# Attention in a float32 kernel: row maxima two heads at a time, sums in spare columns, reciprocals in quarters

## The chip, the cores and the metric

One core of one Trainium2 chip. The metric is the device time of one execution in microseconds; the kernel before has a median of 1218.71 us over three runs (1218.32 to 1220.46).

## What is computed

Attention over 4 batches of 8 heads with queries pooled in pairs, then a gated MLP that mixes positions, then a second MLP behind a low-rank mix of positions. The change lies in the attention:

```python
def _attn_ref(q, k, v) -> np.ndarray:
    B, H, S, D = q.shape          # 4, 8, 1152, 64
    q_pool = q.reshape(B, H, S // 2, 2, D).mean(axis=3)
    scores = (1.0 / np.sqrt(D)) * np.matmul(q_pool, k.transpose(0, 1, 3, 2))
    scores = scores - np.max(scores, axis=-1, keepdims=True)
    attn = np.exp(scores)
    attn = attn / (np.sum(attn, axis=-1, keepdims=True) + 1e-09)
    return np.matmul(attn, v).astype(np.float32)
```

The weights of the MLPs arrive in float64 (w_spatial in float32) and are turned into pairs of float32 parts, high and low, by the kernel itself, during the attention.

## The kernel before, in words

The 32 heads are 16 pairs, and the 576 pooled queries of a pair of heads are two halves of 256 and 320: 32 jobs `u`, in order. A job goes over 9 chunks of 128 keys. Scores are made transposed, keys on the partitions: `scores(u, c)` (L180) writes a tile of two banks, one for each head, with q and k in full float32; `less` (L190) adds the negated row maximum by a matmul with a row of ones; `expo` (L201) exponentiates on ACT (L206) and adds the result up over the chunks on POOL (L211, tile `acc`); `pv` (L215) multiplies with V on PE into one bank for the job. At the end of a job `sums(u)` (L227) sums `acc` over the partitions by matmuls with ones, ACT copies that to SBUF (L238), `recip` (L240) takes the reciprocal on DVE in two halves, `out` (L245) multiplies and stores.

The maximum of a query must be known before its scores are made, so a second, rounded product q k is made ahead of it: `piece()` (L141) is one matmul (L147, 384 keys of one head, 128 queries) into one of the two banks of the pool `ring`, and one maximum over its 384 columns on DVE (L151). Six of them make 128 queries of two heads; a last small minimum (L154) joins them. `to_rows(u)` (L158) turns the columns of maxima into rows by transposing matmuls (L168) into both ring banks, from which ACT copies them (L173, L178). `sums` takes a ring bank too.

Banks of PSUM: 2 for the ring, 2 for the outputs of PV, 2 tiles of 2 for the scores.

The order is written by hand and every engine goes through its own part of it in order. The loop at L277 has 144 groups of two chunks (`G = 2`), nine groups to a pair of heads. A group is: up to two pieces (`some(2)`, L292), scores of both chunks, `less` and `expo` of both, up to two pieces again (L304) or, in the last group before a new job, all pieces that the job still needs and `to_rows` (L298 to L302), PV of the group before, then what is left of an ended job (L311: the sums and the first half of the reciprocal two groups after its last chunk, the second half and the output three groups after), then `also(i)`. `end` (L286) bounds the pieces: `AHEAD` of them ahead of an even rate.

`also(i)` runs one tick of `Weights` (L353): from group 8 on, every sixth group begins one unit of a weight, and each unit does one step a group for seven groups: two activations on ACT (L439, L440), then on DVE L444 and L446, on POOL L448, on DVE L450, then the copy to the high part (L460) and the subtraction for the low part (L465). The strings of `CFG` (L914) give the engines of the last two for each unit: first letter for the subtraction (v DVE, p POOL), second for the copy (v DVE, a ACT). A float32 unit has only these two steps.

After the loop come PV and the sums of the last job, then the two MLPs.

## Time and profile before

| | |
|---|---|
| median of three runs | 1218.71 us |
| the profiled execution's own time | 1220.57 us |
| its span, first to last instruction | 1218.8 us |
| granted clock of PE, mean of full speed | 0.986 |
| PE busy | 1164.7 us (96%) |
| DVE, ACT, POOL busy | 646.3, 438.8, 558.3 us |

The rows below come from the profiled execution. A row of a timeline has the start in us from the start of the span, the duration, the engine (PEld is PE's weight load), the line of the kernel, the operation, the tiles out<-in, the shapes and a count, since neighbours of one kind are merged; in brackets stands the idle time before it and the work whose end ended it. In a group by line stand the count, busy us, mean ns of one, and the idle time before them. The tile `yh` in some rows is room that the rounded q and k and the maxima borrow from a later stage.

### The profile page before, as it was taken

The numbers are of one execution on the slowest core, as the hardware profiler recorded it, in microseconds if no ns is written. First come the engines' busy times: TensorE is split into PE (matmuls) and PEld (weight loads), VectorE is DVE, ScalarE is ACT, GpSimd is POOL, SyncE is SP. The second block draws the span as 40 slices with busy tenths as digits, with TensorE's granted clock in tenths as the row PEclk, the third lists the DMA queues.
The fourth block names the chain that finished last, engine by engine and source line by source line (L and its number), as shares of the span: only waits on it lengthen the run. The fifth ranks groups of instructions, "written<-read, shape, count | busy, mean of one in ns | idle before, by whom it ended". The sixth has DMA issues, their size and how long they took to land.

```text
span 1218.8 us, 18185 instructions
## 1 busy us (share of the span) xinstructions
PE 1164.7 (96%) x7116; PEld 912.9 (75%) x7116; DVE 646.3 (53%) x1158; ACT 438.8 (36%) x868; POOL 558.3 (46%) x458
## 2 busy tenths in 40 slices
PE   7999999999999999999999999789999999999998
PEld 5665656566656555558998989579999999999997
DVE  4677767776777776745434333989852112121211
ACT  2444445444454444444333333555521111111110
POOL 3787878878778877773424243634310000000000
PEclk7999999999999999999999999989999999999999
DMA  6242223223333320001111103624400101010000
GB/s 155 79 106 72 76 82 88 79 79 96 86 99 115 80 59 30 26 15 54 44 40 39 49 1 129 189 98 133 136 27 26 52 1 52 1 52 1 27 1 27
DMA packets 37768, 79.17 MB, mean 65 GB/s; under 512 B 5553, under 2 KB 17841, under 8 KB 37682
## 3 DMA queue, kind: packets, MB, share of 16 engines
q1 hardware_dynamic: 37682, 78.01, 21.6%
q8 instruction: 56, 0.92, 0.3%
q14 instruction: 30, 0.25, 0.1%
HBM read 63.31 MB, written 14.16 MB: 64 GB/s over the span
## 4 chain that ended last, share of the span: by engine, by line
PE 50%; DVE 4%; DMA 0%; ACT 0%; issue 0%; POOL 0%; ACTq 0%; DVEq 0%
PE ph L1006 16%; PE py L1020 16%; PE pu L758 4%; PE pv L623 4%; PE pg L776 4%; PE py L806 3%; DVE w L465 1%; DVE st L450 1%; PE pV L831 1%; PE pt L998 1%; PE pU L792 1%; DVE st L444 1%; DVE st L446 0%; DMA raw<-in_moe_w_ch_dram 0%; DVE yh L345 0%
## 5 line engine op out<-in xcount | busy, mean ns | idle before, releaser
L211 POOL TENSOR_TENSOR acc<-acc,pt 128x512 f32<-128x512 f32 (+1 forms) x222 | 318.1, 1433 | 96.0 <-ACT pt L206 85.3
L151 DVE TENSOR_REDUCE m<-r 128x1 f32<-128x384 f32 x480 | 250.3, 550 | 103.1 <-PE r L147 98.0
L206 ACT ACTIVATE pt<-s 128x512 f32<-128x512 f32 (+1 forms) x288 | 171.6, 648 | 246.5 <-PE s L195 225.2
L1020 PE MATMUL py<-w,h 128*128 128x512 f32 x864 | 218.4, 397 | 1.9 <-ACT h L1009 1.4
L1006 PE MATMUL ph<-ut,w 128*128 128x384 f32 x1152 | 218.4, 338 | 0.0
L1006 PEld LDWEIGHTS ph<-ut,w 128*128 128x128 f32 x1152 | 205.5, 188 | 8.5
L1010 DVE SCALAR_TENSOR_TENSOR h<-ph,h 128x384 fp32r<-128x384 f32 x96 | 53.5, 557 | 267.2 <-ACT h L1009 267.1
L1020 PEld LDWEIGHTS py<-w,h 128*128 128x128 f32 x864 | 160.5, 189 | 32.6 <-ACT h L1009 1.7
L186 PE MATMUL s<-q,k 64*128 64x320 f32 (+1 forms) x1152 | 176.4, 412 | 0.4 <-ACT pt L206 0.4
L222 PE MATMUL po<-pt,v 128*64 128x320 f32 (+1 forms) x1152 | 171.7, 419 | 0.0
L147 PE MATMUL r<-yh 64*128 64x384 f32 x480 | 149.5, 431 | 21.3 <-DVE m L151 11.8
L1009 ACT ACTIVATE h<-ph 128x384 fp32r<-128x384 f32 x96 | 47.2, 491 | 310.9 <-PE ph L1006 310.9
L147 PEld LDWEIGHTS r<-yh 64*128 64x128 f32 x480 | 70.9, 188 | 113.0 <-DVE m L151 73.7
L186 PEld LDWEIGHTS s<-q,k 64*128 64x128 f32 x1152 | 117.2, 189 | 13.0 <-ACT pt L206 2.6
L222 PEld LDWEIGHTS po<-pt,v 128*64 128x64 f32 x1152 | 70.0, 136 | 51.1 <-issue 21.6
L195 PE MATMUL s<-toprow,yh 64*128 64x256 f32 (+1 forms) x576 | 100.7, 405 | 0.0
L243 DVE RECIPROCAL sum<-sum 128x128 f32<-128x128 f32 (+1 forms) x64 | 66.8, 1047 | 52.3 <-ACT sum L238 52.3
L448 POOL TENSOR_TENSOR st<-st,raw 128x512 int32<-128x512 int32 (+3 forms) x48 | 68.8, 1435 | 53.2 <-DVE st L446 43.3
L195 PEld LDWEIGHTS s<-toprow,yh 64*128 64x128 f32 x576 | 64.6, 190 | 11.7 <-issue 0.4
L776 PE MATMUL pg<-wst,vn 128*128 128x288 f32 x448 | 60.1, 295 | 0.0
L776 PEld LDWEIGHTS pg<-wst,vn 128*128 128x128 f32 x448 | 59.6, 188 | 0.0
L211 POOL TENSOR_TENSOR acc<-pt 128x512 f32<-128x512 f32 (+1 forms) x32 | 46.6, 1455 | 25.0 <-ACT pt L206 25.0
(117 smaller groups left out, 1131.2 us busy)
## 6 DMA issues: line engine op xcount, KB each, us to landing
raw<-in_moe_w_ch_dram SPq DMA_DIRECT2D x32, 512.0 KB, 3.8
k<-in_k_dram SPq DMA_DIRECT2D x32, 288.0 KB, 4.5
qraw<-in_q_dram SPq DMA_DIRECT2D x32, 288.0 KB, 5.8
v<-in_v_dram SPq DMA_DIRECT2D x16, 576.0 KB, 4.5
xn<-x SPq DMA_DIRECT2D x4, 1152.0 KB, 5.7
out_dram<-un SPq DMA_DIRECT2D x18, 256.0 KB, 2.1
raw<-in_moe_w_in_dram SPq DMA_DIRECT2D x8, 512.0 KB, 4.6
u<-o SPq DMA_DIRECT2D x16, 256.0 KB, 2.0
```

The lines of the kernel that those rows point to most:

```text
L147: nc.tensor.matmul(r, s["qr"][p, q0:q0 + 128], s["kr"][p, PW * i:PW * i + PW], start=True, stop=True)
L151: nc.vector.tensor_reduce(out=m[:, e, i:i + 1], in_=r, axis=AX.X, op=ALU.max, negate=True)
L186: nc.tensor.matmul(t[:, e, 0:n], s["k"][p, 128 * c:128 * c + 128], s["q"][p, q0:q0 + n], start=True, stop=False)
L195: nc.tensor.matmul(jb["s", c][:, e, 0:n], first[p], jb["top"][p, 0:n], start=False, stop=True)
L206: nc.scalar.activation(x[:, :, 0:n], t[:, :, 0:n], ACTF.Exp, scale=SC)
L211: nc.gpsimd.tensor_tensor(out=a, in0=jb["p", 0][:, :, 0:n] if c == 1 else a, in1=x[:, :, 0:n], op=ALU.add)
L222: nc.tensor.matmul(jb["o"][D * e:D * e + D, 0:n], st[u // 2]["v"][:, e, c], x[:, e, 0:n], start=c == 0, stop=c == KC - 1,)
L243: nc.vector.reciprocal(out=t, in_=t)
L448: nc.gpsimd.tensor_tensor(out=o, in0=o, in1=lo, op=ALU.add)
L776: nc.tensor.matmul(p[:, 0:HT], vn[:, a, s, 128 * m:128 * m + 128], wst[:, c, s, sl], start=s == 0 and i == 0, stop=s == NT - 1 and i == 1,)
L1006: nc.tensor.matmul(p[:, 0:BT], w1s[m][:, a, k], ut[i][:, c, k], start=j == 0, stop=j == 3 * KD - 1)
L1020: nc.tensor.matmul(py[i][c], h[:, a, 128 * c:128 * c + 128], w2s[m][:, e], start=m == 0 and a + e == 0, stop=m == KM - 1 and a == 1,)
```

## The change

One piece is now both heads: two matmuls into a tile of two banks, and one maximum over both (two heads by 384 columns). The ring has one such tile; before the loop the pieces rotate through it and the two score tiles. The transposes of the maxima go into one such tile, and one ACT copy takes both halves. `AHEAD` is 5 pieces of the new kind.

The order within a group: the transposes (and missing pieces), or else one piece; small work of an ended job; scores, `less`, `expo`; one piece; small work; PV; sums; `also`. The sums go into columns 320 and up of the group's second score tile, in two halves of the queries, one a bank, so with twice as many matmuls of half the width. The reciprocal is done in quarters, two in each of the third and fourth group after the last chunk; the output comes in the fifth.

All strings of `CFG` say `pa`: every subtraction on POOL, every copy on ACT (`V0` is not touched).

```diff
--- before.py
+++ after.py
@@ -58,13 +58,13 @@
 
     G = 2
 
-    AHEAD = 7
+    AHEAD = 5
 
     with ExitStack() as ctx, ExitStack() as sco:
         pt_p = ctx.enter_context(tc.tile_pool(name="pt_p", bufs=8))
         ld2 = ctx.enter_context(tc.tile_pool(name="ld2", bufs=2))
         ld = sco.enter_context(tc.tile_pool(name="ld", bufs=2))
-        ring_p = ctx.enter_context(tc.tile_pool(name="ring", bufs=2, space=PSUM))
+        ring_p = ctx.enter_context(tc.tile_pool(name="ring", bufs=1, space=PSUM))
         ps_o = ctx.enter_context(tc.tile_pool(name="ps_o", bufs=2, space=PSUM))
         ps_s = sco.enter_context(tc.tile_pool(name="ps_s", bufs=2, side="right", space=PSUM))
 
@@ -129,27 +129,28 @@
             nc.scalar.copy(s["kr"][:, c0:c1], s["k"][:, c0:c1])
 
         def ring(name):
-            return ring_p.tile([128, 512], F32, tag="r", name=name)
-
-
-        pieces = [
-            (u, c, i, e) for u in range(NJ) for c in range(len(HALF[u % 2][2])) for i in range(NPC) for e in range(2)
-        ]
-        upto = [sum(len(HALF[w % 2][2]) for w in range(u)) * NPC * 2 for u in range(NJ + 1)]
+            return ring_p.tile([128, 2, 512], F32, tag="r", name=name)
+
+
+        pieces = [(u, c, i) for u in range(NJ) for c in range(len(HALF[u % 2][2])) for i in range(NPC)]
+        upto = [sum(len(HALF[w % 2][2]) for w in range(u)) * NPC for u in range(NJ + 1)]
         done = [0]
 
-        def piece():
-            u, c, i, e = pieces[done[0]]
+        def piece(r=None):
+            u, c, i = pieces[done[0]]
             done[0] += 1
             s, q0 = st[u // 2], HALF[u % 2][2][c]
-            p = slice(D * e, D * e + D)
-            r = ring("r")[:, 0:PW]
-            nc.tensor.matmul(r, s["qr"][p, q0:q0 + 128], s["kr"][p, PW * i:PW * i + PW], start=True, stop=True)
-            if i == 0 and e == 0:
+            r = ring("r") if r is None else r
+            for e in range(2):
+                p = slice(D * e, D * e + D)
+                nc.tensor.matmul(
+                    r[:, e, 0:PW], s["qr"][p, q0:q0 + 128], s["kr"][p, PW * i:PW * i + PW], start=True, stop=True
+                )
+            if i == 0:
                 jobs[u]["m"] = ld.tile([128, 2, NPC], F32, tag="m", name="m", bufs=4)
             m = jobs[u]["m"]
-            nc.vector.tensor_reduce(out=m[:, e, i:i + 1], in_=r, axis=AX.X, op=ALU.max, negate=True)
-            if i == NPC - 1 and e:
+            nc.vector.tensor_reduce(out=m[:, :, i], in_=r[:, :, 0:PW], axis=AX.X, op=ALU.max, negate=True)
+            if i == NPC - 1:
                 t = tops[u // 2 % 2][c + 2 * (u % 2)]
                 nc.vector.tensor_reduce(
                     out=t.rearrange("p (e d) -> p e d", e=2)[:, :, 0], in_=m, axis=AX.X, op=ALU.min
@@ -160,22 +161,21 @@
             h = u % 2
             n = HALF[h][1]
             t = jobs[u]["top"] = ld.tile([128, NMAX], F32R, tag="toprow", name="toprow")
-            rs = [ring(f"tr{i}") for i in range(2)]
+            rs = ring("tr")
             for c in range(3 if h else 2):
                 for i in range(2):
                     if c < 2 or i:
                         p = slice(64 * i, 64 * i + 64)
                         nc.tensor.matmul(
-                            rs[i][:, 64 * c:64 * c + 64], tops[u // 2 % 2][c + 2 * h][p], idr[p, p],
+                            rs[:, i, 64 * c:64 * c + 64], tops[u // 2 % 2][c + 2 * h][p], idr[p, p],
                             start=True, stop=True,
                         )
-            for i in range(2):
-                nc.scalar.copy(
-                    t[:, 0:256].rearrange("p (c i x) -> p i c x", c=2, i=2)[:, i],
-                    rs[i][:, 0:128].rearrange("p (c x) -> p c x", c=2),
-                )
+            nc.scalar.copy(
+                t[:, 0:256].rearrange("p (c i x) -> p i c x", c=2, i=2),
+                rs[:, :, 0:128].rearrange("p i (c x) -> p i c x", c=2),
+            )
             if n > 256:
-                nc.scalar.copy(t[:, 256:n], rs[1][:, 128:192])
+                nc.scalar.copy(t[:, 256:n], rs[:, 1, 128:192])
 
         def scores(u, c):
             s = st[u // 2]
@@ -224,22 +224,26 @@
                     start=c == 0, stop=c == KC - 1,
                 )
 
-        def sums(u):
+        def sums(u, r, at):
+
             jb = jobs[u]
-            n = HALF[u % 2][1]
-            r = ring("ps")
+            n = HALF[u % 2][1] // 2
             terms = [jb["p", c] for c in range(added(u), KC)] + [jb["acc"]]
-            for i, x in enumerate(terms):
-                for e in range(2):
-                    nc.tensor.matmul(
-                        r[D * e:D * e + D, 0:n], ones, x[:, e, 0:n], start=i == 0, stop=i == len(terms) - 1
-                    )
+            for h in range(2):
+                for i, x in enumerate(terms):
+                    for e in range(2):
+                        nc.tensor.matmul(
+                            r[D * e:D * e + D, h, at:at + n], ones, x[:, e, n * h:n * h + n],
+                            start=i == 0, stop=i == len(terms) - 1,
+                        )
             t = jb["sum"] = ld2.tile([128, NMAX], F32, tag="sum", name="sum")
-            nc.scalar.activation(t[:, 0:n], r[:, 0:n], ACTF.Copy, bias=1e-9)
+            nc.scalar.activation(
+                t[:, 0:2 * n].rearrange("p (h n) -> p h n", h=2), r[:, :, at:at + n], ACTF.Copy, bias=1e-9
+            )
 
         def recip(u, i):
             n = HALF[u % 2][1]
-            t = jobs[u]["sum"][:, n * i // 2:n * (i + 1) // 2]
+            t = jobs[u]["sum"][:, n * i // 4:n * (i + 1) // 4]
             nc.vector.reciprocal(out=t, in_=t)
 
         def out(u):
@@ -259,21 +263,30 @@
 
         r = ring("warm")
         for i in range(WARM):
-            nc.tensor.transpose(r[:, 128 * (i % 4):128 * (i % 4) + 128], idf, idf)
+            nc.tensor.transpose(r[:, 0, 128 * (i % 4):128 * (i % 4) + 128], idf, idf)
         pool_q(0, nc.vector, 0, 256)
         round_q(0, 0, 256)
         round_k(0)
         pool_q(0, nc.gpsimd, 256, T)
         round_q(0, 256, T)
-        for _ in range(upto[1]):
-            piece()
+        for i in range(upto[1]):
+            piece(ps_s.tile([128, 2, 512], F32, tag="s", name="r0") if i % 3 else None)
         pool_q(1, nc.gpsimd)
         to_rows(0)
         chunks = [(u, c) for u in range(NJ) for c in range(KC)]
         groups = [chunks[i:i + G] for i in range(0, len(chunks), G)]
         PG = 2 * KC // G
         before = []
-        waiting = []
+
+        smalls = {}
+        sums_at = {}
+        for i, group in enumerate(groups):
+            for u, c in group:
+                if c == KC - 1 and u < NJ - 1:
+                    sums_at[i + 2] = u
+                    for n in range(4):
+                        smalls[i + 3 + n // 2, n % 2] = [lambda u=u, n=n: recip(u, n)]
+                    smalls[i + 5, 0] = [lambda u=u: out(u)]
         for i, group in enumerate(groups):
             j, r = divmod(i, PG)
             if r == 0:
@@ -285,37 +298,36 @@
 
             end = min(upto[1] + AHEAD + upto[2] * (i + 1) // PG, upto[NJ])
 
-            def some(n):
-                for _ in range(min(n, end - done[0])):
+            def some():
+                if done[0] < end:
                     piece()
 
-            some(2)
-            for u, c in group:
-                scores(u, c)
-            for u, c in group:
-                less(u, c)
-                expo(u, c)
             new = [u for u, c in (groups[i + 1] if i + 1 < len(groups) else ()) if c == 0]
             for u in new:
                 while done[0] < upto[u + 1]:
                     piece()
                 to_rows(u)
             if not new:
-                some(2)
+                some()
+            for x in smalls.pop((i, 0), ()):
+                x()
+            for u, c in group:
+                scores(u, c)
+            last = jobs[group[-1][0]]["s", group[-1][1]]
+            for u, c in group:
+                less(u, c)
+                expo(u, c)
+            some()
+            for x in smalls.pop((i, 1), ()):
+                x()
             if i + 1 == len(groups):
                 break
             for x in before:
                 pv(*x)
             before = group
 
-            for u, n in waiting:
-                if n == 1:
-                    sums(u)
-                    recip(u, 0)
-                if n == 2:
-                    recip(u, 1)
-                    out(u)
-            waiting = [(u, n + 1) for u, n in waiting if n < 2] + [(u, 0) for u, c in group if c == KC - 1]
+            if i in sums_at:
+                sums(sums_at[i], last, NMAX)
             also(i)
             if r == 4 and j + 2 < NP:
                 pool_q(j + 2, nc.gpsimd)
@@ -331,8 +343,10 @@
             pv(*x)
             for name in names.split():
                 also(name)
-        sums(NJ - 1)
-        for i in range(2):
+        for x in [x for k in sorted(smalls) for x in smalls[k]]:
+            x()
+        sums(NJ - 1, ring("ps"), 0)
+        for i in range(4):
             recip(NJ - 1, i)
         out(NJ - 1)
         for name in LEFT[G].split():
@@ -912,11 +926,11 @@
 
 
 CFG = dict(
-    EI="pa vv va pv va pv pa pa",
-    ES="va pa pa vv va",
-    EW="pa pv pv pa",
-    EU="pv pa",
-    EV="va pv",
+    EI="pa pa pa pa pa pa pa pa",
+    ES="pa pa pa pa pa",
+    EW="pa pa pa pa",
+    EU="pa pa",
+    EV="pa pa",
     V0="pv pv vv vv pa",
     END=[1, 3, 2, 2, 0, 2, 2, 1, 1, 3, 4, 2, 6],
     START="D D D D U D U n U n U n U n U n U n U n b U U U U U U U U U " + "X " * 9 + "G " * 17 + "P " * 9,
```

## Rows read from the trace of the kernel before

**Rows 1.** Stretch, us, busy us (instructions) of PE, PEld, DVE, ACT, POOL; clock, DMA.
```profile
53.41:521.62 468.21, 437.86 (x3181) 279.33 (x3181) 341.65 (x638) 219.25 (x424) 373.39 (x270) 1.00 0.29 81
```

**Rows 2.** Timeline, PE, first scores of a group: start, us, engine, line, operation.
```profile
255.34 1.02 PE L186 MATMUL s<-q,k 64*128 64x256 f32 x7
...
258.69 1.02 PE L186 MATMUL s<-q,k 64*128 64x256 f32 x8
...
262.50 1.13 PE L186 MATMUL s<-q,k 64*128 64x256 f32 x7
...
266.22 1.02 PE L186 MATMUL s<-q,k 64*128 64x256 f32 x8
...
270.09 1.13 PE L186 MATMUL s<-q,k 64*128 64x256 f32 x8
...
273.03 1.26 PE L186 MATMUL s<-q,k 64*128 64x320 f32 x8
...
276.26 1.24 PE L186 MATMUL s<-q,k 64*128 64x320 f32 x8
...
280.11 1.34 PE L186 MATMUL s<-q,k 64*128 64x320 f32 x7
...
286.69 1.02 PE L186 MATMUL s<-q,k 64*128 64x256 f32 x7
```

**Rows 3.** Timeline of a group 4, of the round from 286.69.
```profile
301.16 0.44 PE L147 MATMUL r<-yh 64*128 64x384 f32 x2
...
301.64 1.02 DVE L151 TENSOR_REDUCE m<-r 128x1 f32<-128x384 f32 x2 [2.00 <-PE r L147]
...
302.68 0.47 PE L147 MATMUL r<-yh 64*128 64x384 f32 x2
...
303.08 0.63 PEld L222 LDWEIGHTS po<-pt,v 128*64 128x64 f32 x8 [0.18 <-issue]
...
304.10 0.22 PEld L147 LDWEIGHTS r<-yh 64*128 64x128 f32 x2 [0.39 <-DVE m L151]
```

**Rows 4.** Timeline of groups 2 and 3 of that round.
```profile
294.89 2.05 DVE L151 TENSOR_REDUCE m<-r 128x1 f32<-128x384 f32 x4
...
295.44 0.18 PEld L147 LDWEIGHTS r<-yh 64*128 64x128 f32 x1 [0.27 <-DVE m L151]
...
299.70 0.52 PE L168 MATMUL tr<-yh 64*128 64x64 f32 x4 [0.36 <-DVE m L151]
```

**Rows 5.** Timeline at the end of its group 6: sums, then maxima.
```profile
310.37 0.60 PE L234 MATMUL ps<-acc,ones 128*64 128x256 f32 x4
...
310.90 0.99 PE L147 MATMUL r<-yh 64*128 64x384 f32 x2
...
311.45 0.18 PEld L147 LDWEIGHTS r<-yh 64*128 64x128 f32 x1 [0.37 <-ACT sum L238]
```

**Rows 6.** Groups of DVE by line, 50 to 535: xcount, busy us, mean ns, idle.
```profile
L151 DVE TENSOR_REDUCE m<-r 128x1 f32<-128x384 f32 x435 | 227.3, 550 | 89.3 <-PE r L147 85.8
L243 DVE RECIPROCAL sum<-sum 128x160 f32<-128x160 f32 x30 | 34.5, 1148 | 16.8 <-ACT sum L238 16.8
L243 DVE RECIPROCAL sum<-sum 128x128 f32<-128x128 f32 x29 | 27.5, 948 | 18.7 <-ACT sum L238 18.7
L450 DVE SCALAR_TENSOR_TENSOR st<-raw,st 128x512 int32<-128x512 int32 x12 | 16.6, 1384 | 2.4 <-POOL st L448 2.4
...
L446 DVE TENSOR_SCALAR st<-st 128x512 int32<-128x512 int32 x12 | 8.0, 669 | 0.0
L444 DVE TENSOR_SCALAR st<-st 128x512 f32<-128x512 f32 x12 | 7.9, 662 | 0.4 <-ACT st L439 0.4
L249 DVE TENSOR_TENSOR x<-po,sum 128x320 f32<-128x320 f32 x15 | 7.4, 492 | 0.5
```

**Rows 7.** Stretch 50 to 535: L465 on DVE and POOL; L460 on DVE and ACT.
```profile
50.00:535.00 485.00, 8.37 (x7) 16.42 (x16) 1.00 0.29 79
...
50.00:535.00 485.00, 6.63 (x9) 7.75 (x14) 1.00 0.29 79
```

## The prediction

> **What bounds the kernel now.** I read the busy time of whole stretches first [rows 1]. In 53.41 to 521.62 us, fourteen of the sixteen rounds of attention (a round is one pair of heads, nine groups of two key chunks), PE is busy for 437.86 of 468.21 us, POOL for 373.39 and DVE for 341.65. What follows attention is not touched by the change. So the time is PE's; what can be won are waits of PE inside attention, and a us won there moves everything behind it by a us.
>
> Next the timeline of PE alone, reduced to the first score matmul of each group [rows 2]. The round from 255.34 to 286.69, in which DVE does no weight work, takes 31.35 us; its groups 0 to 6 take 3.35, 3.81, 3.72, 3.87, 2.94, 3.23 and 3.85, groups 7 and 8 together 6.58. Group 4 has full work of its kind (four maxima, eight scores, eight PV) in 2.94, so 3.7 to 3.9 in groups 2 and 3 must hold waits. The timelines of such places name them. In group 2 four maxima queue on DVE behind half a reciprocal, and PE's weight load stands behind a maximum at 295.44; in group 3 the transposes of the maxima wait for them [rows 4]. In groups 1 and 6 the sums are made in one of the two banks of the maxima: the second maximum's matmul gets it only when ACT has copied them out, 0.55 us after the place where the sums ended [rows 5]. Over the fourteen rounds the mean is 468.21/14 = 33.44, 2.09 above the quiet round: weight work on DVE, put in front of maxima, costs 29 us in all.
>
> **The maxima.** Before: two matmuls into two banks, two maxima of 550 ns, 1.02 us for the two in a row [rows 3, 6]. After: one of 768 columns. Bounds: above 1.02, as now; below 0.90, since from 320 columns (492 ns, another operation from PSUM) to 384 (550) a column costs 0.91 ns [rows 6]. I take 0.95: nearer to the row of the same operation, 550 and 384 columns more at a little over 1 ns. In exchange there is one tile of two banks where there were two of one. Its next matmul waits for the whole maximum: start at 0.48 us behind the first matmul, as now, to 0.59, as it must now await the second (half of the 0.22 that two weight loads take); then 0.95; then the 0.02 between 302.66 and 302.68 [rows 3]. So a pair follows a pair at the earliest after C = 1.57 us (bounds 1.40 and 1.63). Now the places of a group lie 1.52 and 1.42 apart [rows 3]: C is a new floor of 3.14 under each group that has two pairs, 0.2 above group 4 as it is.
>
> [...]
>
> **Placement.** The list gives 15 pairs a round. Groups 3 and 8, ahead of a new half, skip the first place, and group 6 finds its count reached at the second; groups 0, 1, 2, 4, 5 and 7 have two pairs. The transposes go from the end of such a group to its start, a group after their last maximum, so they await only the tile. ACT's copy of them, now ahead of the exponentials in ACT's queue, has the scores as cover, most of the 1.52 between two places [rows 3]; without it the next pair would wait some 0.5 us for the tile, twice a round.
>
> **Sums.** Four matmuls in 0.53 us become eight of half width: 0.53 if columns count, 1.06 if matmuls do; eight weight loads of 64 columns took 0.63 [rows 3, 5], and I take that. What waits for ACT afterwards is the second score tile of the next group, behind a pair and the first tile's scores, an estimated 0.7 of the 1.52 from place to place, where ACT's copy released after 0.55: hidden; without that cover 0.4 us in each of 31 halves.
>
> **Reciprocals.** 948 ns at 128 columns, 1148 at 160, so 6.25 ns a column [rows 6]: quarters of 64 and 80 take 0.55 and 0.65, 0.3 us more a half in all. DVE, paced by C, has C - 0.95 = 0.62 us free behind each maximum, so a quarter fits where a half of 1.15 did not; if the gap is shorter, its excess goes to PE. The products, one group later, ride in the same gap; their store on SP waits behind them, with nothing but loads due rounds later in its queue.
>
> **The round, then.** Group 0: 3.2 (floor, longer PV). Group 1: 1.57 to its second place, then 1.42 and 0.63 for the sums: 3.63. Group 2: floor and a late quarter, 3.25. Group 3: one pair for two, transposes for the other, then the floor to the next place: 3.2. Group 4: 3.17 (a loss of 0.23). Group 5: 3.23, unchanged. Group 6: 3.85 less the wait of 0.4, plus 0.1: 3.55. Groups 7 and 8: 6.64. Sum 29.87, against 31.35: 1.48 less, in some 15 rounds **22 us**. With C at 1.40 the round falls to about 29.1 (12 us more won); at 1.63, to 30.4 (8 us less); with sums at 1.06, 13 us less.
>
> **Weights.** The changed strings take every subtraction (8.37 us) and copy (6.63) from DVE, to POOL and ACT [rows 7]. They are 15.0 us beside the 16.6, 8.0 and 7.9 of the three that stay (L450, L446, L444 [rows 6]), 32% of the 29: 9 us. Of what stays, a third follows a group with a single pair, where DVE is free, and 0.62 us of each of the others hides: of 20 us I keep 14. Together **15 us**; bounds 8 (nothing of what stays hides) and 25. On POOL the 7 subtractions come to about 7 us at its own durations (16 took 16.42 [rows 7]): it would be busy for 380 of some 431 us, 88%; the adds of the next group queue behind them, and PE waits for those only if they come two groups late, at the sums. On ACT, busy for 219.25 [rows 1], nine copies more of 0.55 (14 took 7.75 [rows 7]) cost nothing: its exponentials wait for PE; without that one would be late by a copy.
>
> **Start.** With five pairs ahead instead of seven singles (a lead of 3.5 pairs) but two places a group instead of four singles, the lead is not there by the first new half: three pairs in a row cost up to 3 x (1.57 less their own matmuls, some 0.3) = 3.8 us in group 3 of the first round. In front, six maxima rotate through three tiles and save at least 6 x 0.07 (0.95 for 1.02). I take a loss of **2 us** (0 to 4).
>
> Sum: -22 - 15 + 2 = -35 from the profiled execution's 1220.57, which stands 1.86 above the median shown: 1185.6 there, **1184** as a median.
>
> **Rivals.**
> *The lockstep decides, and it gets slower.* Place: the one tile of maxima, PE to DVE and back. If the maximum over two banks costs more than the two it replaces, each 0.1 us of C costs about 0.1 in eleven intervals a round, 16 us. From C = 1.78 (a maximum of 1.16) the 35 us are eaten; at 1.9 the time is 1238. Against: the two in a row took 1.02 [rows 3], and nothing shows that one could take more. For: all the weight work left on DVE then hits with its full length. [...] Chance 0.10.
> *POOL binds.* With 88% and bursts (a subtraction and an integer add within one group) the running sum comes late, the sums wait for it, and L450 holds DVE until POOL's add is through (2.4 us over its 12 times now [rows 6]). If that returns all that the weights were to give, 1199. Against: the mean is below 1. Chance 0.13.
> *The waits only move.* Quarters and products do not fit the gap, or the sums' tile is late: each round wins half, 1201. Chance 0.20.
> *More is won:* the maximum at 0.90 with C near 1.40, little left of the collisions: 1168. Chance 0.10.
> My forecast, 1174 to 1194, has 0.47.
>
> **Numbers.** A measurement of this kernel tells 0.2%, 2.4 us, from none. Only the first rival is slower; of its 0.10 and the tails of POOL's case I give slower 0.11, same 0.04, faster 0.85. From 1168 (C, weights at their best) to 1212 (C at 1.63, sums at 1.06 and weights at 8 together) lie all cases but the lockstep and the ends of the others.
>
> **What would show it.** Right: maxima of 0.95 us, 240 of them; group 2 at about 3.25 and group 3 at 3.2, where no transpose awaits DVE; group 4 slower than now, near 3.15; no wait of maxima for ACT's sums; quarters of 0.55 and 0.65 with no idle PE behind; POOL at 88%, its adds before the sums. Wrong: a maximum above 1.1, matmuls of scores waiting for ACT's sums, sums awaiting POOL, or groups with L444, L446 and L450 as long as now.

## The result and the profile after

The changed kernel takes **1198.88 us** (median of four runs, 1198.58 to 1199.07), the kernel before took 1219.59 beside it (1218.32 to 1222.27): a ratio of 0.9827 with a 95% interval of 0.9809 to 0.9845. It is faster, as forecast, and inside the outer range of 1168 to 1212, but above the 1174 to 1194 that was called the forecast: 20.7 us are won where the sum said 35. The time is that of the rival "POOL binds", 1199; how far its reasons came true is told below.

First the page's groups of instructions of the changed kernel (line, engine, operation, count; busy us and mean ns; idle time before it and what ended it). They answer to [rows 6], with line numbers of the changed kernel: the maximum is L152, the reciprocal L247, and L444, L446, L448 and L450 have become L458, L460, L462 and L464.

```profile
L152 DVE TENSOR_REDUCE m<-r 128x2 f32<-128x768 f32 x240 | 229.3, 957 | 119.4 <-PE r L146 117.5
...
L247 DVE RECIPROCAL sum<-sum 128x64 f32<-128x64 f32 (+1 forms) x128 | 71.6, 580 | 15.9 <-ACT sum L240 15.6
...
L464 DVE SCALAR_TENSOR_TENSOR st<-raw,st 128x512 int32<-128x512 int32 (+3 forms) x48 | 50.1, 1043 | 22.9 <-POOL st L462 22.9
```

The last row is the one to stop at: DVE stood idle for 22.9 us ahead of L464, until POOL's integer add L462 was through. In the kernel before it stood for 3.6, all of it ahead of the 44 that have 512 columns:

```profile
L450 DVE SCALAR_TENSOR_TENSOR st<-raw,st 128x512 int32<-128x512 int32 x44 | 41.4, 941 | 3.6 <-POOL st L448 3.6
```

Next the busy time of stretches (columns as in [rows 1]): the same fourteen rounds, then the quiet round, then two pieces of one long group that are read below.

```profile
56.20:501.26 445.06, 406.81 (x3294) 255.99 (x3294) 323.41 (x469) 220.36 (x405) 380.24 (x276) 0.98 0.29 82
254.35:283.18 28.83, 28.44 (x239) 17.98 (x239) 19.75 (x31) 14.51 (x26) 25.78 (x19) 1.00 0.37 98
223.37:227.77 4.40, 1.26 (x14) 0.95 (x12) 2.60 (x2) 1.08 (x2) 4.32 (x4) 1.00 0.81 226
227.77:231.58 3.81, 3.81 (x21) 2.28 (x22) 0.96 (x1) 0.16 (x1) 1.47 (x2) 0.55 0.29 78
```

In the quiet round PE is busy for 28.44 of 28.83 us: almost nothing is left to win in it. In the fourteen rounds it is busy for 406.81 of 445.06, so some 38 us of waits lie where there is weight work. The rounds are counted from 0. With the stretches between first scores, the span comes apart like this:

| stretch | before | after | difference | forecast |
|---|---|---|---|---|
| to the first scores | 20.40 | 18.30 | -2.1 | start, with the row below: +2 |
| first round | 33.01 | 37.90 | +4.9 | |
| rounds 1 to 14, each at the length of the quiet round | 438.9 | 403.6 | -35.3 | -1.48 a round |
| rounds 1 to 14, what they take beyond that | 29.3 | 41.4 | +12.1 | -15 |
| last round, to the end of its last scores | 26.3 | 24.3 | -2.0 | -1.48 |
| behind those | 670.9 | 671.4 | +0.5 | 0 |

But for rounding, the differences add up to the 21.8 between the spans (1218.8 and 1197.0). The round gained 2.52 us where 1.48 were forecast; the **collisions with weight work**, forecast to lose half of their 29 us, grew to 41.

The quiet round, group by group, from PE's timeline (first scores of a group, as in [rows 2]):

```profile
254.35 1.02 PE L186 MATMUL s<-q,k 64*128 64x256 f32 x8
...
257.45 1.03 PE L186 MATMUL s<-q,k 64*128 64x256 f32 x8
...
260.90 1.03 PE L186 MATMUL s<-q,k 64*128 64x256 f32 x8
...
264.01 0.46 PE L186 MATMUL s<-q,k 64*128 64x256 f32 x1
...
266.99 1.14 PE L186 MATMUL s<-q,k 64*128 64x256 f32 x8
...
270.00 1.24 PE L186 MATMUL s<-q,k 64*128 64x320 f32 x8
...
273.04 1.24 PE L186 MATMUL s<-q,k 64*128 64x320 f32 x8
...
276.84 1.24 PE L186 MATMUL s<-q,k 64*128 64x320 f32 x8
...
279.95 1.32 PE L186 MATMUL s<-q,k 64*128 64x320 f32 x8
...
283.18 1.02 PE L186 MATMUL s<-q,k 64*128 64x256 f32 x8
```

Groups 0 to 8 take 3.10, 3.45, 3.11, 2.98, 3.01, 3.04, 3.80, 3.11 and 3.23. Groups 2 and 3, at 3.72 and 3.87 before, are now as short as the others. The pace of the maxima shows in group 4 (all engines):

```profile
266.71 0.45 PE L146 MATMUL r<-yh 64*128 64x384 f32 x2
...
267.20 0.96 DVE L152 TENSOR_REDUCE m<-r 128x2 f32<-128x768 f32 x1
...
268.21 0.19 PEld L146 LDWEIGHTS r<-yh 64*128 64x128 f32 x2
```

From pair to pair it is 1.50 us: 0.49 to the maximum, 0.96 for it, 0.05 behind it. The next stretch of the same timeline is a group 1 with weight work, in round 6, 8.21 us long where the quiet one took 3.45:

```profile
215.55 8.30 POOL L211 TENSOR_TENSOR acc<-acc,pt 128x640 f32<-128x640 f32 x5
...
217.21 0.36 DVE L460 TENSOR_SCALAR st<-st 128x512 int32<-128x512 int32 x1
...
223.79 1.29 POOL L462 TENSOR_TENSOR st<-st,raw 128x512 int32<-128x512 int32 x1
...
225.04 1.26 POOL L211 TENSOR_TENSOR acc<-pt 128x512 f32<-128x512 f32 x1
225.12 1.73 DVE L464 SCALAR_TENSOR_TENSOR st<-raw,st 128x512 int32<-128x512 int32 x1 [1.99 <-POOL st L462]
...
226.77 0.94 DVE L152 TENSOR_REDUCE m<-r 128x2 f32<-128x768 f32 x1
...
227.77 0.69 PE L146 MATMUL r<-yh 64*128 64x384 f32 x2 [3.14 <-DVE m L152]
...
228.39 1.98 PE L222 MATMUL po<-pt,v 128*64 128x256 f32 x8
```

What L462 adds is ready at 217.57, with the end of L460, but POOL reaches it only at 223.79, at the end of an unbroken run of five adds of the running sum. DVE has L464 at the head of its queue and stands for 1.99 us; the maximum of group 1's first pair, whose matmuls began at 223.09, stands behind it until 226.77; PE has one tile for maxima and stands for 3.14. After that idle time PE is granted 0.55 of its clock as a mean of 3.81 us (the window from 227.77 above), and eight PV matmuls take 1.98 where they take 1.08 in group 1 of the quiet round. Of the 4.76 us that the group lost, 3.14 are the wait; the other 1.62 are about what the window lost by its clock, 3.81 x 0.45 = 1.7 by my estimate. The waits over 50 to 500 us (us in total, times, longest):

```profile
PE r L146 <- DVE m L152: 30.2, 23, 3.2
...
DVE st L464 <- POOL st L462: 21.7, 11, 2.5
...
PEld s L235 <- POOL acc L211: 9.4, 14, 0.7
```

The first of these rows in the kernel before:

```profile
PE r L147 <- DVE m L151: 8.5, 20, 0.8
```

Before, no wait of PE for the room of a maximum was over 0.8 us; now there are some of over 3. Group 1 lasted 6.6 to 8.2 us in rounds 2, 4, 6, 10 and 12, and group 7, 3.11 in the quiet round, 4.64 to 4.66 in rounds 2, 4 and 10. In these eight groups eight of the twelve wide L464 wait for 2.0 to 2.5 us, and together they are 25 us longer than the same groups of the quiet round: 25 of the 41.4. Elsewhere DVE's own weight work got longer. The twelve L458, 662 ns each before (L444 in [rows 6]), now take 1337, and a group 4 with weight work takes up to 4.26 for 3.01. The last row of the waits is the running sum coming late to the sums: the weight load waits up to 0.7 for it, while PE still works.

### The profile page after: what moved, and what is told of

Same layout as the page of the kernel before. It is cut to its first block, busy times and chain, and to the rows that moved or that the text cites. A ratio compares the mean times of both kernels' runs of the same rounds, so it can differ in the third digit from the quotient of the medians.

```text
span 1197.0 us, 18244 instructions
## 1 busy us (share of the span) xinstructions
PE 1130.7 (94%) x7252; PEld 887.6 (74%) x7252; DVE 625.8 (52%) x966; ACT 440.1 (37%) x845; POOL 566.1 (47%) x465
## 4 chain that ended last, share of the span: by engine, by line
PE 73%; DVE 11%; POOL 7%; issue 4%; ACT 2%; DMA 2%; SPq 0%; POOLq 0%; ACTq 0%; DVEq 0%
PE ph L1020 17%; PE py L1034 16%; PE po L222 8%; PE s L186 7%; POOL acc L211 6%; PE r L146 5%; PE pu L772 4%; DVE m L152 4%; PE pv L637 4%; PE pg L790 4%; PE py L820 3%; DVE st L464 3%; PE s L195 2%; POOL st L462 1%; DVE w L479 1%
## 5 line engine op out<-in xcount | busy, mean ns | idle before, releaser
L211 POOL TENSOR_TENSOR acc<-acc,pt 128x512 f32<-128x512 f32 (+1 forms) x222 | 318.1, 1433 | 68.0 <-ACT pt L206 55.4
L152 DVE TENSOR_REDUCE m<-r 128x2 f32<-128x768 f32 x240 | 229.3, 957 | 119.4 <-PE r L146 117.5
L222 PE MATMUL po<-pt,v 128*64 128x320 f32 (+1 forms) x1152 | 175.0, 425 | 0.0
L186 PE MATMUL s<-q,k 64*128 64x320 f32 (+1 forms) x1152 | 172.4, 416 | 0.0
L146 PE MATMUL r<-yh 64*128 64x384 f32 x480 | 104.7, 427 | 42.5 <-DVE m L152 34.1
L146 PEld LDWEIGHTS r<-yh 64*128 64x128 f32 x480 | 48.5, 192 | 100.6 <-DVE m L152 82.3
L186 PEld LDWEIGHTS s<-q,k 64*128 64x128 f32 x1152 | 110.0, 192 | 16.9 <-ACT pt L206 1.8
L195 PE MATMUL s<-toprow,yh 64*128 64x256 f32 (+1 forms) x576 | 96.5, 407 | 0.0
L462 POOL TENSOR_TENSOR st<-st,raw 128x512 int32<-128x512 int32 (+3 forms) x48 | 68.8, 1435 | 53.2 <-DVE st L460 43.3
L247 DVE RECIPROCAL sum<-sum 128x64 f32<-128x64 f32 (+1 forms) x128 | 71.6, 580 | 15.9 <-ACT sum L240 15.6
L195 PEld LDWEIGHTS s<-toprow,yh 64*128 64x128 f32 x576 | 58.4, 192 | 15.5
L464 DVE SCALAR_TENSOR_TENSOR st<-raw,st 128x512 int32<-128x512 int32 (+3 forms) x48 | 50.1, 1043 | 22.9 <-POOL st L462 22.9
```

The costliest lines, as they stand in the source:

```text
L146: nc.tensor.matmul(r[:, e, 0:PW], s["qr"][p, q0:q0 + 128], s["kr"][p, PW * i:PW * i + PW], start=True, stop=True)
L152: nc.vector.tensor_reduce(out=m[:, :, i], in_=r[:, :, 0:PW], axis=AX.X, op=ALU.max, negate=True)
L186: nc.tensor.matmul(t[:, e, 0:n], s["k"][p, 128 * c:128 * c + 128], s["q"][p, q0:q0 + n], start=True, stop=False)
L195: nc.tensor.matmul(jb["s", c][:, e, 0:n], first[p], jb["top"][p, 0:n], start=False, stop=True)
L211: nc.gpsimd.tensor_tensor(out=a, in0=jb["p", 0][:, :, 0:n] if c == 1 else a, in1=x[:, :, 0:n], op=ALU.add)
L222: nc.tensor.matmul(jb["o"][D * e:D * e + D, 0:n], st[u // 2]["v"][:, e, c], x[:, e, 0:n], start=c == 0, stop=c == KC - 1,)
```

## The experiments

Two readings were open. Either the handing over costs: L464 comes one group behind POOL's L462, which was far enough in the longer groups of before and is too near now. Or POOL itself has too much to do, because of the subtractions that the new strings give it. Two things can be set apart in the first: how many groups L464 is behind L462, and in which groups of the round it falls.

**e1_late_combine.** The combining of the two words comes one tick later, two groups behind POOL's add; the steps after it follow.

```diff
-                if phase < 7:
-                    self.work(u, phase)
-                if phase == (6 if u["f32"] else 4) and "own" not in u and i != self.keep:
+                late = self.apart == 6 and not u["f32"]
+                if phase < 7 + late:
+                    self.work(u, phase - 1 if late and phase > 4 else 9 if late and phase == 4 else phase)
+                if phase == (6 if u["f32"] else 4 + late) and "own" not in u and i != self.keep:
...
-        while self.begun <= last or self.time - self.units[last]["begun"] < 7:
+        while self.begun <= last or self.time - self.units[last]["begun"] < 7 + (self.apart == 6):
```

> The changed kernel, but of each float64 weight the combining step on DVE (L464) comes two groups after POOL's integer add (L462) instead of one, and the two steps behind it one group later. Theory A (DVE, held by L464 until POOL's add is through, is what the change lost): the groups 1 of 6.6 to 8.2 us in rounds 2, 4, 6, 10, 12 fall to 3.5 to 4.5 and the groups 7 of 4.65 to 3.1, L464 waits for POOL for under 3 us in all (21.7 now), 1179 to 1184 us. Rival B (the subtractions that the strings put on POOL are the burden): POOL is as full as now, PE waits for it elsewhere, 1196 to 1201. Rival C (the length of L464 itself in front of a maximum, not its wait): it hits another group instead, 1190 to 1196.

Measured: 1165.99 us, ratio to before 0.9551 [0.9537, 0.9565], 33 us under the changed kernel. The stretch of the fourteen rounds, then DVE's line of the combining over 50 to 500 us (now L465), then the place that answers to the one above:

```profile
56.66:468.21 411.55, 399.48 (x3294) 251.90 (x3292) 309.97 (x469) 220.24 (x405) 381.37 (x276) 1.00 0.32 89
```
```profile
L465 DVE SCALAR_TENSOR_TENSOR st<-raw,st 128x512 int32<-128x512 int32 x12 | 11.6, 963 | 0.0
```

The same row of the changed kernel:

```profile
L464 DVE SCALAR_TENSOR_TENSOR st<-raw,st 128x512 int32<-128x512 int32 x12 | 20.0, 1666 | 17.5 <-POOL st L462 17.5
```

The place:

```profile
209.14 1.30 POOL L463 TENSOR_TENSOR st<-st,raw 128x512 int32<-128x512 int32 x1
...
210.40 1.27 POOL L211 TENSOR_TENSOR acc<-pt 128x512 f32<-128x512 f32 x1
...
211.01 1.21 DVE L465 SCALAR_TENSOR_TENSOR st<-raw,st 128x512 int32<-128x512 int32 x1
```

No wait for POOL is left (idle 0.0, before it 17.5 for the same twelve), the granted clock is 1.00, and the collisions are down to 411.55 - 14 x 28.80 (its own quiet round) = 8.3 us. POOL has the same work, 381.37 us, in 33 us less: 93% busy and not in the way. So POOL's load was not the bound; the wait for one of its instructions was. The gain is larger than expected even by the theory that it bears out, and 8 us larger than what the eight groups with the long waits had lost. The steps behind L464 moved too and L464 falls into other groups, so this run alone does not say how much the wait was worth.

**e2_old_strings.** The strings of before in the changed kernel (only the first of five lines shown).

```diff
-    EI="pa pa pa pa pa pa pa pa",
+    EI="pa vv va pv va pv pa pa",
...
```

> The changed kernel with the strings of the kernel before: 7 subtractions and 9 copies back on DVE. Theory A (POOL's integer add is late because of the adds of the running sum, which the faster rounds crowd): the waits of L464 stay at 15 us or more, DVE has 15 us more to do in front of maxima, 1199 to 1208 us. Rival B (the moved subtractions make POOL late): the long groups 1 and 7 go, 1180 to 1190.

Measured: 1199.63 us, 0.982 [0.9802, 0.9838]; L464 waits for POOL for 20.8 us, 11 times. With seven subtractions fewer on POOL L464 waits as before, so the load that the strings moved is not what delays L462; and in this kernel the strings are worth 0.8 us, less than the spread of these runs.

**e3_max_by_head.** Maxima per head again, from the same tile.

```diff
-            nc.vector.tensor_reduce(out=m[:, :, i], in_=r[:, :, 0:PW], axis=AX.X, op=ALU.max, negate=True)
+            for e in range(2):
+                nc.vector.tensor_reduce(out=m[:, e, i:i + 1], in_=r[:, e, 0:PW], axis=AX.X, op=ALU.max, negate=True)
```

> The changed kernel with one maximum for each head (two instructions of 384 columns) out of the one tile of two banks. If the merged maximum is worth its fixed share: about 1.02 to 1.06 us for 0.96, so places 1.56 to 1.6 apart for 1.50, the quiet round 29.4 to 30 for 28.83, 1208 to 1215 us. If the order of the work alone carries the gain: the quiet round within 0.2 of 28.83, 1198 to 1202.

Measured: 1205.23 us, 0.9874 [0.9855, 0.9894], 6.4 more than the changed kernel, between the two times expected. Its quiet round, the first scores of it and of the next one:

```profile
257.49 1.03 PE L187 MATMUL s<-q,k 64*128 64x256 f32 x8
...
286.75 1.02 PE L187 MATMUL s<-q,k 64*128 64x256 f32 x8
```

It takes 29.26, so the merged maximum is worth 0.43 us a round; two maxima in a row take 1.02, and pairs follow each other after 1.56 instead of 1.50. In fifteen rounds that makes the 6.4, though the runs lie 5.6 apart (1202.31 to 1207.87).

**e4_nine_ahead.** Nine pairs ahead of the first round instead of six.

```diff
-        for i in range(upto[1]):
+        for i in range(upto[1] + 3):
```

> The changed kernel with nine pairs of maxima ahead of the loop instead of six. If the three pairs in a row of the first round (group 2, 7.66 us against 3.10 in a quiet round, and the low clock of the group behind it) are a loss of the lead: the first group comes some 2.9 us later and the first round falls from 37.9 to 31 to 33 us, 1195 to 1197.5 us. Rival: DVE is as busy in front as it was later, and the time is the same within 1 us.

Measured: 1193.29 us, 0.9778 [0.9761, 0.9794], 5.6 less, more than expected. First scores at 19.63 instead of 18.30, first round 30.35 instead of 37.90. What the lead costs in front, 1.3, it gives back more than five times. The first round of the changed kernel shows why:

```profile
29.71 0.44 PE L146 MATMUL r<-yh 64*128 64x384 f32 x2
31.21 0.44 PE L146 MATMUL r<-yh 64*128 64x384 f32 x2 [1.06 <-DVE m L152]
32.71 0.44 PE L146 MATMUL r<-yh 64*128 64x384 f32 x2 [1.06 <-DVE m L152]
34.21 0.64 PE L169 MATMUL tr<-yh 64*128 64x64 f32 x4 [1.06 <-DVE m L152]
```

Three pairs in a row, 1.50 apart, with PE idle for 1.06 behind each.

**e5_recip_halves.** Reciprocals in halves, in the places of the first and third quarter.

```diff
-            t = jobs[u]["sum"][:, n * i // 4:n * (i + 1) // 4]
-            nc.vector.reciprocal(out=t, in_=t)
+            if i % 2 == 0:
+                t = jobs[u]["sum"][:, n * i // 4:n * (i + 2) // 4]
+                nc.vector.reciprocal(out=t, in_=t)
```

> The changed kernel with the reciprocal in halves again, one behind the first maximum of each of the two groups. If quarters matter because they fit the gap that the lockstep leaves (1.50 less 0.96): the half of 1.15 pushes the second maximum of group 2 by some 0.6 us, that of 0.95 the one of group 7 by 0.3; groups 3 and 8 have one pair and hide theirs; the quiet round 29.6 to 29.8 for 28.83, 1209 to 1214 us. If they only cost their fixed share: the quiet round as it is, 1197 to 1200.

Measured: 1197.84 us, 0.9822 [0.9807, 0.9837], no different from the changed kernel. Its quiet round is 0.43 longer, in group 2, where a half does not fit the gap between maxima:

```profile
260.33 1.14 DVE L248 RECIPROCAL sum<-sum 128x160 f32<-128x160 f32 x1
...
261.39 0.90 DVE L152 TENSOR_REDUCE m<-r 128x2 f32<-128x768 f32 x1
...
262.34 0.41 PE L169 MATMUL tr<-yh 64*128 64x64 f32 x4 [0.47 <-DVE m L152]
```

But rounds 1 to 14 take 444.09, as much as in the changed kernel (445.06): over all rounds halves lose nothing; why the others make up for the quiet round no run shows. The quarters do what they are for in the quiet round alone, and no time came of it here. Whether they do with the late combining was not tried.

**e6_sums_in_ring.** Sums in the tile of the maxima again.

```diff
-                sums(sums_at[i], last, NMAX)
+                sums(sums_at[i], ring("ps"), 0)
```

> The changed kernel with the sums in the tile of the maxima instead of spare columns of a score tile. If the spare columns took the wait for ACT's copy off PE: the first pair of groups 2 and 7 waits 0.4 to 0.5 us for ACT, while group 6 gains up to 0.3, since its sums no longer await the exponential of the same banks: the quiet round 29.3 to 29.8 for 28.83, 1204 to 1212 us. If the wait was hidden either way: 1197 to 1200.

Measured: 1212.55 us, 0.9929 [0.9906, 0.9952], 13.7 more than the changed kernel. Its waits, and the timeline at the end of a group 1:

```profile
PE r L146 <- ACT sum L240: 14.1, 28, 0.5
```
```profile
265.12 0.44 PE L146 MATMUL r<-yh 64*128 64x384 f32 x2 [0.53 <-ACT sum L240]
```

The maxima wait for ACT's copy of the sums, 28 times in the stretch, and PE stands idle for it 14.1 us in all. Time and quiet round (29.82) come out just above what the first theory expected; group 6 did not gain, it takes 3.96 for 3.80. If the parts simply add up, the spare columns hold 1.0 of the 2.52 us that the quiet round gained, the merged maximum 0.43 and the quarters 0.43. The rest, some 0.66, would belong to the order (transposes at the start of a group, the lead of five pairs), which was not tried alone.

**b_late_combine.** The edit of e1_late_combine in the kernel before.

```diff
-                if phase < 7:
-                    self.work(u, phase)
...
+                if phase < 7 + late:
+                    self.work(u, phase - 1 if late and phase > 4 else 9 if late and phase == 4 else phase)
...
```

> The kernel before, with L450 two groups behind POOL's add instead of one. If L450's hold of DVE is a loss that the change brought by crowding POOL: it waits 2.4 us in all here, so little is won, 1212 to 1218 us. If it was there before in hiding (its 1.75 us beside POOL's adds, 1.2 us in the groups 1): 1204 to 1211.

Measured: 1226.14 us, 1.0052 [1.0037, 1.0067], slower. Rounds 1 to 14 take 472.16 instead of 468.21, the quiet one as before. A wait of 2.4 us could not give much; that it loses was expected by neither theory. L451 (L450 before) fell from a mean of 1384 ns to 1018, but L447 (L446 before) rose from 669 to 1074, twelve times each. The groups 1 of rounds 2, 4, 6 and 12 fell from 5.0 us to 3.8, so the hand-over did cost some 1.2 in each of them already in the kernel before; but the groups 8 of rounds 1, 3, 5 and 11 rose from 3.7 to 5.0, and others by less. The steps hold DVE in other groups now, and the rounds got 3.95 us longer in all; how much of this is the distance and how much the new places was not tried here. What holds is that the edit that won 33 us in the changed kernel wins nothing in the one before.

**b_new_strings** and **best_old_strings.** The strings alone, in the kernel before, and the old strings in the best version (below; here as a diff against that one).

```diff
-    EI="pa vv va pv va pv pa pa",
+    EI="pa pa pa pa pa pa pa pa",
...
```
```diff
-    EI="pa pa pa pa pa pa pa pa",
+    EI="pa vv va pv va pv pa pa",
...
```

> The kernel before with the strings of the change alone: subtractions to POOL, copies to ACT. If copies and subtractions cost what the prediction's step gave them (9 of the 29 us of collisions): 1208 to 1213 us. If what DVE no longer does comes back as L450's wait for a fuller POOL: within 3 us of the kernel before.

> The kernel with L464 one group later and nine pairs ahead, with the strings of the kernel before. If the strings are worth their 9 us once L464 no longer holds DVE: 1164 to 1171 us. If the gap of the lockstep hides copies and subtractions on DVE as well as on POOL: 1157 to 1161.

Measured: 1213.66 us, 0.9954 [0.9935, 0.9973], and 1172.78, 0.961 [0.9592, 0.9627]. The strings give 7.0 us to the kernel before (rounds 1 to 14: 7.8 less), 0.8 to the changed one, and 1172.78 - 1158.84 = 13.9 to the best version, more than either theory had it.

**e7_shift_one** and **e8_late_old_place.** These set distance and place apart, the place being that of all steps of a unit and not of L464 alone. WEIGHTS is the group at which the weight units begin: in e7 every step comes a group later, L464 still one group behind L462; e8 has the edit of e1 and begins a group earlier, so that L464 is two groups behind and falls where it fell in the changed kernel, at the ends of groups 0, 3 and 6.

```diff
-WEIGHTS = 8
+WEIGHTS = 9
```
```diff
-WEIGHTS = 8
+WEIGHTS = 7
```

> The changed kernel with the weights begun one group later: L464 still one group behind POOL's add (L462), but at the ends of groups 1, 4 and 7, where e1_late_combine has it, and L462 at the ends of 0, 3 and 6. Distance theory: L464 still waits for POOL, at other groups, and the time stays well above 1166, 1180 to 1200 us. Place theory (what e1_late_combine won came from moving L464 off the ends of groups 0, 3 and 6): 1163 to 1172, with next to no wait of L464.

> The kernel e1_late_combine with the weights begun one group earlier: L464 two groups behind POOL's add, but at the ends of groups 0, 3 and 6 as in the changed kernel. Distance theory: no wait of L464, groups 1 at 3.5 to 4.5 us, 1164 to 1173 us. Place theory: the groups 1 are long again, 1185 to 1200.

Measured: 1185.23 us, 0.97 [0.9685, 0.9714], and 1179.09, 0.9653 [0.9637, 0.9669]. Together with the two kernels that they lie between:

| L464 behind L462 by | ends of groups 0, 3, 6 | ends of groups 1, 4, 7 |
|---|---|---|
| one group | 1198.88 (changed kernel) | 1185.23 (e7) |
| two groups | 1179.09 (e8) | 1165.99 (e1) |

Distance is worth 19.8 and 19.2 us, the place 13.7 and 13.1. By the ratios to the kernel before, which ran beside each of them, it is 21.2 and 18.2, 15.5 and 12.4. In e7 L464's wait is short, though the distance is one group:

```profile
DVE st L464 <- POOL st L462: 2.9, 7, 0.5
```
```profile
199.87 0.36 DVE L460 TENSOR_SCALAR st<-st 128x512 int32<-128x512 int32 x1
...
204.45 1.30 POOL L462 TENSOR_TENSOR st<-st,raw 128x512 int32<-128x512 int32 x1
...
205.78 1.74 DVE L464 SCALAR_TENSOR_TENSOR st<-raw,st 128x512 int32<-128x512 int32 x1 [0.46 <-POOL st L462]
```

So the wait is not a matter of distance alone. POOL lags more or less when it comes to L462, by the place in the round: here L462 begins 4.22 us after the end of L460, in the long group of the changed kernel above 6.22. Over the twelve wide units it is 2.6 to 4.6 in e7, 4.9 to 6.2 in the changed kernel and 3.4 to 5.0 in the kernel before. e7 also has a loss of its own, 8.9 us in group 1 of round 1: the first raw weights arrived late. ACT waited for the transfer:

```profile
67.67 0.66 ACT L453 ACTIVATE st<-raw 128x512 f32<-128x512 f32 x1 [8.42 <-DMA raw<-in_moe_w_in_dram]
```

Without it e7 would stand near 1176, the place would be worth some 22 us at one group's distance, and distance some 10 at the later place; the table's even sums are partly chance. In e8 the combining waits for POOL no more, but another wait is there, PE's for ACT's rounding of k, which stands in ACT's queue behind a weight's activations (at 92 to 94 us, for one):

```profile
PE r L146 <- ACT yh L129: 8.0, 6, 1.7
```

In the changed kernel it was 2.1 us. So part of what the table calls the place is not L464's.

**best_late_nine.** The edits of e1_late_combine and e4_nine_ahead together, in the changed kernel.

```diff
+                late = self.apart == 6 and not u["f32"]
...
+        for i in range(upto[1] + 3):
```

> The changed kernel with both edits, L464 one group later and nine pairs ahead of the loop. If the two losses are apart: 1165.99 less the 5.6 of the nine pairs, 1159.5 to 1162 us, with a first round near 30.4 and no group 1 over 4.3. If POOL, now more crowded still, pushes back: 1163 to 1167.

Measured: **1158.84 us** (1157.32 to 1160.33), 0.9503 [0.9487, 0.952]: 40 us under the changed kernel, 61 under before. Rounds 1 to 14 of it:

```profile
50.40:461.96 411.56, 399.45 (x3292) 251.85 (x3292) 310.12 (x469) 220.25 (x405) 381.39 (x276) 1.00 0.32 88
```

PE is busy for 97% of them and POOL for 93%.

## Why the prediction was right and wrong

**Right: maxima and pace.** 240 maxima of 0.957 us (forecast 0.95), and a pace of 1.50 us (forecast 1.57), in the lower half of the bounds of 1.40 and 1.63. The maximum does not start later for having to await the second matmul: 0.49, where it was 0.48, so the 0.59 from which the 1.57 was summed did not come. Group 4 lost 0.07, not 0.23. The rival by which the lockstep makes it slower fell with this. With one tile, where two banks took turns before, the group that had no other wait takes 3.01 for 2.94, and 3.12 in e3, where the maximum is not merged. So there is a loss, but the 0.07 are small beside the 2.52 us that the round gained, and the change as a whole does not lose by it.

**Right: placement and gap.** Groups 2 and 3 came to 3.11 and 2.98 (3.25 and 3.2 forecast); a quarter of a reciprocal fits behind a maximum (0.64 us at 262.18, and the maximum behind it begins 0.49 after its matmuls, as in group 4), and e5 shows that a half does not (1.14 at 260.33, and 0.98). That this would turn into time at the end did not follow: e5 takes as long.

**Off: the sums.** Groups 1 and 6 were forecast at 3.63 and 3.55 and came at 3.45 and 3.80. The wait of 0.4 in group 6 is gone, but the group was full: PE was busy in it for 3.73 of 3.85 us before, and is for 3.63 of 3.80 now (before, then after; the quiet round of each).

```profile
276.26:280.11 3.85, 3.73 (x29) 2.06 (x28) 1.76 (x5) 1.69 (x3) 3.77 (x4) 1.00 0.00 0
```
```profile
273.04:276.84 3.80, 3.63 (x33) 2.16 (x33) 0.96 (x1) 1.47 (x3) 3.72 (x4) 1.00 0.00 0
```

The wait was that of a weight load, and PE was idle for only 0.12 in the whole group before; the step counted the wait as idle PE. The load, at the end of that group:

```profile
280.11 0.18 PEld L147 LDWEIGHTS r<-yh 64*128 64x128 f32 x1 [0.37 <-ACT sum L238]
```

A new wait is in the rest:

```profile
275.97 0.66 PE L235 MATMUL s<-acc,ones 128*64 128x128 f32 x8 [0.17 <-ACT pt L206]
```

The sums share their banks with the last scores, and here they wait 0.17 for the exponential that reads those. The step overlooked this wait; whether it is kept for the bank or for the whole tile the row does not tell.

**Mis-sized: the round.** 28.83 us instead of 29.87, with every group but 6 below its forecast, even below the 29.1 that the prediction gave for C at 1.40. Of the 1.04, C itself is about 0.32, by the prediction's own scale (0.77 for 0.17 of C, of which 0.07 came). The rest lies in terms that were not the floor: group 1 by 0.18, group 3, which has one pair, by 0.22, and groups 7 and 8, which the sum left almost as they were, by 0.30. The lower end of the range was not summed from its own terms either: 12 us for C and 10 for the weights under 1184 make 1162 and not 1168.

**Wrong: the weights.** The failing step is that of the adds on POOL: "PE waits for those only if they come two groups late, at the sums". It priced the load on POOL (380 us, measured 380.24) and left out the place where DVE takes a result back from POOL. The two adds of a wide group, one of 320 queries, take 2 x 1.58 us on POOL; such a group took 3.2 to 3.9 before, and POOL began L462 3.4 to 5.0 us after DVE had made it ready. With groups of 3.0 to 3.2, but for the sixth, POOL lags more (4.9 to 6.2 at L462), L464 stands at the head of DVE's queue, and the maxima, behind which PE is in lockstep, stand with it. The sign of the term turned: 29.3 us of collisions became 41.4 and not 14. The groups with the long waits hold 25 of the 41.4; e1 takes the wait away (33 us back, 8.3 of collisions left), e2 shows that the moved load does not make it, and e7 and e8 that some 20 us of the 33 belong to the distance (at the later place perhaps only 10) and the rest to the place. Two of the prediction's signs of being wrong came: the sums awaited POOL, if only with their weight loads, and the groups with L464 got longer and not shorter.

The mechanism stood in the document as a part of the rival "POOL binds" ("L450 holds DVE until POOL's add is through"), at 0.13 and with the time that came, 1199. That the time agrees is luck: the rival left the collisions at 29 us and the round at its forecast, while the collisions grew by 12.1 and the fourteen rounds won 35.3 otherwise, where 14 x 1.48 = 20.7 were forecast. For the same reason the whole was out by 15 us only, where the weights alone were out by 27. The argument against the rival, that POOL's mean is below 1, is none for a queue in order: it was 0.85 in the changed kernel's fourteen rounds (380.24 of 445.06), and L464 waited all the same; nor is a high mean one for it, since e1 runs at 93% without the wait.

**The strings.** Forecast 9 us, measured 7.0 in the kernel before, 0.8 in the changed one and 13.9 in the best. The price was fair. That the wait for POOL hid it in the changed kernel is how I read it; no run shows it by itself.

**Start.** Forecast +2, measured +2.8, by the mechanism named: three pairs in a row. The sum is closer than its parts: -2.1 in front, where at least -0.4 was counted, and +4.9 in the first round, where 3.8 was the most. What the step left out is the clock that PE was granted there, 0.66 as a mean from 30 to 40 us.

## What to carry to other kernels

When a loop gets shorter, look again at each result that one engine takes from another a fixed number of steps later: the distance that was nearly enough at the old length may not be, and what stands behind the taker in its engine's queue comes late with it (here a maximum, 3.68 us after its matmuls began instead of 0.49). Ask for a mean below 1 and also for the place in the round where the giver is furthest behind. In a lockstep of two engines price waits on both, and count a wait of weight loads as a gain only where PE is idle by the stretch's busy time.

## What was not expected of the hardware

The combining lasts 1.73 us in the changed kernel's place above and 1.21 in e1's, and both end at the same distance behind POOL's add: 225.12 + 1.73 = 226.85 is 0.55 after 225.04 + 1.26, and 211.01 + 1.21 = 212.22 is 0.55 after 210.40 + 1.27. So its end hung on POOL's add and not on its own start; six of e1's twelve took 0.63 to 0.68. The twelve of the changed kernel all do the same: each began 0.07 to 0.80 us after the start of an add of the running sum (L211) and ended 0.54 to 0.56 after its end. In the kernel before there is the reverse as well: three combinings of 0.63 to 0.68, at 114.90, 355.31 and 378.94, began within 0.08 of the start of such an add, and there the adds took 2.10, 1.82 and 2.10, where others of their widths take 1.55 and 1.27. The second of the three:

```profile
355.31 1.82 POOL L211 TENSOR_TENSOR acc<-pt 128x512 f32<-128x512 f32 x1 [0.32 <-ACT pt L206]
355.31 0.68 DVE L450 SCALAR_TENSOR_TENSOR st<-raw,st 128x512 int32<-128x512 int32 x1
```

So where the two met in these rows, either the combining ended some 0.55 behind the add or the add took some 0.55 longer; what they share, and which of them stands back, the rows do not tell. The eight combinings that L462 released began 0.07 to 0.09 after the start of POOL's next add and took 1.73 to 2.02; the mean of the twelve is 1666 ns in the changed kernel, 963 in e1. The kernel before had this already, with 1384 [rows 6].

The other is the clock behind a long wait of PE: after the 3.14 us it was 0.55 as a mean of the next 3.81 us, and the group lost 1.62 more than the wait. Of the four other waits of 3.15 or 3.16 us for the room of a maximum, three were followed by 0.55, 0.71 and 0.65 over as long a window, and one, at 348.85, by 1.00; behind the eight waits of 1.03 to 1.28 us in the fourteen rounds it was 1.00. From what length of wait on the clock falls, and why it did not at 348.85, no run shows.
